# Recurrences of the first two batches on 16x16 blocks, with a block level on TensorE and layout changes by DVE transposes

## The chip, the cores and the metric

The kernel runs on one core of one Trainium2 chip. The metric is the device time in microseconds: the median over several runs of the same program. One of the executions is recorded by the hardware profiler, and every row quoted from the profile or the trace comes from that execution. PE is TensorE's matmuls (PEld its weight loads), DVE VectorE, ACT ScalarE, POOL GpSimd, and SP the engine whose queue issues all DMAs of this kernel (SPq).

## The reference

Two stages, in fp32. The first is a delta rule over 768 positions for 4 batches and 8 heads of dimension 48; the second is a feed-forward layer on its output (3072 tokens, 384 to 1024 to 384), with a SoLU activation and a layer norm.

```python
k_n = k / (np.linalg.norm(k, axis=-1, keepdims=True) + 1e-06)
for t in range(S):
    kt, vt, bt = (k_n[:, :, t], v[:, :, t], beta[:, :, t, None])
    y[:, :, t] = np.einsum('bhd,bhde->bhe', q[:, :, t], state)
    v_old = np.einsum('bhde,bhd->bhe', state, kt)
    state = state + bt[:, :, :, None] * np.einsum('bhd,bhe->bhde', kt, vt - v_old)
```
```python
h = x @ w_in
e = np.exp(h - h_max)
solu = h * e / (np.sum(e) + 1e-09)
ln = (solu - mu) / np.sqrt(var + 1e-06) * g_ln
out = ln @ w_out
```

## The kernel before

**Tiles.** The 768 positions are cut into 12 chunks of 64. A *unit* is one chunk for one pair of batch entries (two entries on 128 lanes, 8 heads side by side), so there are 24 units, numbered in the order in which the state passes through them. Within a chunk the recurrence is the inverse of a triangular 64x64 matrix per head and batch entry, made of the products of the keys (the gram). The inverses of several units are made together: what the title calls a batch (m in the code, `NB = 7` of them) holds two units (m = 0, chunk 0), four units (m = 1 to 5, two chunks) or two units (m = 6, chunk 11). Batch 2 therefore starts with unit 6.

**One batch.** `gram` multiplies a unit's keys with themselves and with the queries on PE (tiles gram and qk in PSUM, tag "fl", two buffers); ACT copies the gram to SBUF (g), DVE masks the queries' part (pm). g goes to DRAM (gd). `to_inv` gathers it back by strided DMAs into ginv, so that each of the 128 lanes holds one 32x32 diagonal block (lane = batch entry, half of the chunk, unit and head). `norms` takes the keys' norms with small DVE operations, `inv_begin` scales the blocks and keeps their triangle (DVE, then a select on POOL), and `inv_step` runs the recurrence, 30 steps of two elementwise operations (itmp, y) over the block. For m = 0 and 1 the columns of each step are divided between DVE (the first ten) and POOL; from m = 2 on POOL does all of it. `inv_end` copies y transposed on ACT (ginv again), stores both forms in DRAM (zd, xd) and gathers them back into the layout that PE needs (zt, gx, gy). `tlevel` with `block_level` joins two 32x32 inverses into a 64x64 one with small matmuls (mps, msb).

**One unit after that.** `chain` multiplies the state with keys and queries (kps, yps), forms the residual r, applies the inverse (ups, from zt) and updates the state (cps) and the output y. y times 64 is split into two fp16 parts (xh on ACT, xl on DVE), and each part is transposed by a DMA (xth, xtl). `moe_h` is 18 matmuls on the fp16 parts of x and w_in (h), the softmax-like activation, and two more DMA transposes (pth, ptl); `moe_out` is 24 matmuls with w_out's parts (ops), a correction and the store. The weights come as 8-byte floats: `to_f32` converts them by integer operations on DVE and products on POOL, six blocks of w_in and eight of w_out, and each block is split into two fp16 parts.

**What sets the order.** Nothing is issued as the Python runs. A `Recorder` collects all operations with a priority (the time given to `add` in the last part of the kernel, plus a shift), an assumed duration and their dependences. `Recorder.order` then plays the program through: an engine that is free takes, of the operations that are ready by the planner's clock, the one with the lowest priority value; a tile is taken from its ring (p1 to p10 are pools of 1 to 10 buffers per tag) when its first operation is placed. The resulting order per engine is fixed, and each engine works it off in order. SP is one such engine: the planner gives a DMA 5 ns per KB. Rings that matter here: kq and pm have ten buffers, kv four, the raw w_in blocks share three with pr, ginv, y and gx have two, and gy one. The gram of batch 2 is held behind the last level recorded before it (`last0`).

Of the kernel before, what the change touches and what calls it, by code (L numbers as in the profile page):

```python
# [20 lines left out]
CH = 1  # L21
SC = 64.0
# [265 lines left out]
class Queue:  # L288
# [17 lines left out]
def kernel(  # L306
# [128 lines left out]
    kqt, kvt, ztx, gxt = {}, {}, {}, {}  # L435
# [61 lines left out]

    def gram(m, u, t0):
# [3 lines left out]
        g = p2.tile([P, H, C], F32, tag="g", name=f"g_{ch}_{bp}")  # L502
# [26 lines left out]
    ginv, yt = {}, {}  # L529
    last0 = [None]  # L530

    def to_inv(m):
        gi = p2.tile([P, 32, 32], F32, tag="ginv", name=f"ginv_{m}")
        ginv[m] = gi
        for b in range(4):
            blk = b % 2
            for z in range(1 if len(units(m)) == 4 else 2):
                src = gdt[m].rearrange("t u h j -> t (u h) j")
                n = H * len(units(m))
                ls = slice(0, n)  # L540
                sp.dma_start(
                    kb=128, out=gi[32 * b + 16 * z : 32 * b + 16 * z + n],
                    in_=src[32 * b : 32 * b + 32, ls, blk * 32 : blk * 32 + 32].rearrange("j l i -> l j i"),
                )
# [384 lines left out]
```

## Time and profile before

| what | value |
|---|---|
| median of 3 runs | 512.82 us (512.18 to 515.02) |
| profiled execution | 512.04 us, of which the span is 510.2 us |
| mean granted TensorE clock | 0.92 |
| busy: PE, DVE, POOL, ACT | 368.2, 318.6, 294.0, 192.9 us |
| DMA | 72.21 MB, 142 GB/s in the mean |

The span runs from the first to the last instruction of the program; the 1.8 us around it are not seen in the trace. The recurrences are the groups named y and itmp; since a helper records every operation, nearly all rows carry the same line (L265), and groups are told apart by tile names. A row of the timeline has start, length, engine, line, operation, tiles and shapes, a count, and in brackets the idle time of the engine before it with what ended it.

### The profile page before, as it was taken

How to read it: one execution, taken by the hardware profiler on the slowest of the kernel's cores; microseconds unless marked ns; L12 is line 12 of the kernel's file. 1: busy time of each engine (PE TensorE's matmuls, PEld its weight loads, DVE VectorE, ACT ScalarE, POOL GpSimd, SP SyncE). 2: the span in 40 equal slices, each digit the busy share in tenths (PEclk: the TensorE clock that was granted, in tenths of full speed). 3: DMA queues.
4: the chain of work that ended last, by engine and by line, in shares of the span. 5: the costliest groups of instructions: out<-in, count | busy, mean ns of one | idle time of the engine just before them, and what ended most of it. 6: DMA issues, size and time to landing. Idle time of an engine off the chain costs nothing.

```text
span 510.2 us, 18246 instructions
## 1 busy us (share of the span) xinstructions
PE 368.2 (72%) x7744; PEld 233.9 (46%) x7744; DVE 318.6 (62%) x791; ACT 192.9 (38%) x382; POOL 294.0 (58%) x506
## 2 busy tenths in 40 slices
PE   3510070689579488997598997787969797899974
PEld 3410070455346345665366564444635464566532
DVE  3599999887884383655088664256597355455670
ACT  2210241465522143536144544224345345454450
POOL 3378385966558998984016886008989898100000
PEclk9999999877876699998799998898989899999998
DMA  8685662987989949977999587985656866744332
GB/s 212 159 255 98 155 169 65 161 171 174 172 162 165 179 113 160 168 135 161 189 165 144 145 162 151 160 162 95 107 118 144 145 114 128 131 64 99 73 68 61
DMA packets 180640, 72.21 MB, mean 142 GB/s; under 512 B 165520, under 2 KB 168976, under 8 KB 180560
## 3 DMA queue, kind: packets, MB, share of 16 engines
q1 hardware_dynamic: 180560, 71.06, 70.8%
q8 instruction: 60, 0.98, 0.9%
q14 instruction: 20, 0.16, 0.1%
HBM read 37.21 MB, written 16.52 MB: 105 GB/s over the span
## 4 chain that ended last, share of the span: by engine, by line
POOL 28%; PE 22%; DVE 19%; issue 10%; DMA 9%; SPq 7%; ACT 4%; POOLq 0%; DVEq 0%; ACTq 0%
POOL y L265 13%; POOL itmp L265 11%; PE h L265 7%; SPq L265 7%; PE ops L265 7%; DVE y L265 5%; DVE itmp L265 4%; DMA zt<-zd 3%; DMA ginv<-gd 3%; PE mps L265 2%; DVE wf L265 2%; DVE rst L265 1%; DVE st L265 1%; PE kps L265 1%; PE yps L265 1%
## 5 line engine op out<-in xcount | busy, mean ns | idle before, releaser
L265 POOL TENSOR_TENSOR y<-y,itmp 128x84 f32<-128x84 f32 (+16 forms) x190 | 100.7, 530 | 14.6
L265 POOL TENSOR_TENSOR itmp<-y,ginv 128x84 f32<-128x84 f32 (+16 forms) x190 | 93.3, 491 | 14.0
L265 DVE TENSOR_REDUCE st<-h 128x1 f32<-128x1024 f32 x24 | 29.3, 1222 | 87.5 <-PE h L265 82.2
L265 PE MATMUL qk<-kq 48*64 48x64 f32 x768 | 40.4, 269 | 24.9 <-DVE pm L265 15.6
L265 PE MATMUL gram<-kq 48*64 48x64 f32 x768 | 43.2, 270 | 18.8 <-DMA kq<-kq_dram 11.5
L265 POOL TENSOR_TENSOR st<-st,nhalf 128x1 f32<-128x1 f32 x24 | 13.2, 551 | 64.1 <-DVE st L265 64.1
L265 PEld LDWEIGHTS gram<-kq 48*64 48x64 f32 x768 | 37.5, 178 | 25.7 <-ACT g L265 6.3
L265 PEld LDWEIGHTS <-pth 128*128 128x128 f16 x384 | 37.6, 99 | 25.5 <-issue 1.7
L265 PE MATMUL h<-win_hi,xtl 128*128 128x512 f16 x144 | 45.4, 419 | 5.3 <-DVE pr L265 2.6
L265 PE MATMUL mps<-zt,gx 32*32 32x32 f32 x768 | 13.5, 205 | 48.6 <-issue 28.9
L265 PE MATMUL h<-win_lo,xth 128*128 128x512 f16 x144 | 46.7, 421 | 1.7 <-POOL win_lo L265 1.7
L265 PEld LDWEIGHTS qk<-kq 48*64 48x64 f32 x768 | 35.8, 178 | 25.3 <-DVE pm L265 16.1
L265 PEld LDWEIGHTS <-xth 128*128 128x128 f16 x288 | 28.4, 105 | 39.7 <-issue 14.8
L265 PE MATMUL ops<-wout_hi,ptl 128*128 128x384 f16 x192 | 38.7, 345 | 8.7 <-DMA ptl<-pl 6.8
L265 PE MATMUL h<-win_hi,xth 128*128 128x512 f16 x144 | 43.4, 411 | 0.0
L265 ACT ACTIVATE e<-h,st 128x1024 f32<-128x1024 f32 x24 | 26.7, 1114 | 38.0 <-DVE st L265 26.4
L265 POOL TENSOR_SCALAR_AFFINE_SELECT y<-y 128x1024 f32<-128x1024 f32 x7 | 9.4, 1346 | 53.5 <-DVE y L265 53.5
L265 DVE TENSOR_SCALAR st<-st 128x1 f32<-128x1 f32 (+1 forms) x216 | 35.5, 165 | 5.6
L265 PE MATMUL ops<-wout_lo,pth 128*128 128x384 f16 x192 | 36.9, 334 | 0.0
L265 PEld LDWEIGHTS mps<-zt,gx 32*32 32x32 f32 x768 | 10.1, 117 | 56.9 <-issue 34.8
L265 PE MATMUL ops<-wout_hi,pth 128*128 128x384 f16 x192 | 35.5, 326 | 0.0
L265 PE MATMUL cps<-u,kv 64*64 64x48 f32 x704 | 28.9, 235 | 9.1 <-ACT u L265 3.2
(94 smaller groups left out, 860.4 us busy)
## 6 DMA issues: line engine op xcount, KB each, us to landing
kq<-kq_dram SPq DMA_DIRECT2D x48, 192.0 KB, 4.5
kv<-kv_dram SPq DMA_DIRECT2D x24, 384.0 KB, 4.3
gd<-g SPq DMA_DIRECT2D x48, 128.0 KB, 3.3
out_dram<-oc SPq DMA_DIRECT2D x24, 192.0 KB, 2.2
zd<-y SPq DMA_DIRECT2D x7, 512.0 KB, 2.6
wi<-w_in_dram SPq DMA_DIRECT2D x6, 512.0 KB, 4.4
wo<-w_out_dram SPq DMA_DIRECT2D x8, 384.0 KB, 4.0
ginv<-gd SPq DMA_DIRECT2D x20, 128.0 KB, 4.2
```

Source lines behind the costliest of these rows:

```text
L265: fn(*[real(a) for a in args], **{k: real(a) for k, a in kw.items()})
```

## The change

For m < `SPLIT` = 2 the 32x32 block is worked as two 16x16 blocks, one on DVE and one on POOL at the same time (`blocks`), in 14 steps. The joining 16x16 block is made by PE: the gram is computed in three 32x32 parts, the layout changes gram to ginv, y to zt and ginv to gy are DVE transposes in place of stores to DRAM and gathers, and a new `small_level` joins two 16x16 inverses before `block_level` joins the 32x32 ones. From m = 2 on the recurrence stays on POOL with DRAM, but g is stored with one DMA instead of two; batch 6 zeroes ginv and gathers 16 lanes instead of 32 per quarter. The gram of batch 2 is not held any more. The two fp16 parts of x are written to one tile and transposed by one DMA. The planner now gives a DMA at least 550 ns and a DMA transpose at least 1,400 ns, and the priorities of the first two batches move: everything of batch 0 forward, the gram and loads of batch 1 right behind it, the kv loads of both ahead of w_in.

```diff
+SPLIT = 2
-        return self.rec.add(self.name, self.engine.dma_start, (), kw, kb * 5.0, 2000)
+        return self.rec.add(self.name, self.engine.dma_start, (), kw, max(550.0, kb * 5.0), 2000)
-        return self.rec.add(self.name, self.engine.dma_start_transpose, (), kw, kb * 5.0, 2000)
+        return self.rec.add(self.name, self.engine.dma_start_transpose, (), kw, max(1400.0, kb * 5.0), 2500)
...
     def gram(m, u, t0):
-        if m == 2:
-            rec.after = last0[0]
+                    if near:
+                        for r, a, b, o in ((0, lo, lo, lo), (32, up, up, lo), (32, up, lo, up)):
+                            pe.matmul(ns=25, out=gps_[C * b2 + r : C * b2 + r + 32, h, o], lhsT=kk[:, a], rhs=kk[:, b], ...)
+                    else:
+                        pe.matmul(ns=60, out=gps_[half(1 - b2), h], lhsT=kk, rhs=kk, start=True, stop=True)
+        if near:
+            hs = slice(H * u, H * u + H)
+            act.copy(out=gct[m][:, hs], in_=gps_[:, :, lo])
+            for r in (32, 96):
+                act.copy(out=gxt[m][0][r : r + 32, hs], in_=gps_[r : r + 32, :, up])
-        for b2 in range(2):
-            sp.dma_start(kb=128, out=gdt[m][half(b2), u], in_=g[half(1 - b2)])
+        sp.dma_start(kb=256, out=gdt[m][:, u], in_=g)
...
     def to_inv(m):
+        if m < SPLIT:
+            dve.transpose(ns=1900, out=gi.rearrange("l j i -> l i j"), in_=gct[m].rearrange("j l i -> j i l"))
+            return
...
+    def blocks(m):
+        return [(dve, slice(0, 16)), (gps, slice(16, 32))] if m < SPLIT else [(gps, slice(0, 32))]
     def inv_step(m, j):
-        parts = [(gps, 0, j)] if m > 1 else [(dve, 0, min(j, 10)), (gps, 10, j)]
+        for eng, q in blocks(m):
+            y, b = yt[m][:, q, q], ginv[m][:, q, q]
+            n = q.stop - q.start - 1 - j
...
     def inv_end(m):
+        if m < SPLIT:
+            act.copy(n=256, out=x1[:, 0:16, 16:32], in_=y[:, 0:16, 0:16].rearrange("p i j -> p j i"))
+            for q in (0, 16):
+                gps.memset(x1[:, q : q + 16, q : q + 16], 0.0)
+            dve.transpose(ns=1900, out=zz[:, :, 32:64].rearrange("p l i -> p i l"), in_=y.rearrange("l j i -> l i j"))
+            dve.transpose(ns=1900, out=xy[:, 0:1024].rearrange("p (l i) -> p i l", i=32), in_=x1.rearrange("l j i -> l i j"))
+            return
...
+    def small_level(u, nm, zz, z0, gx, xy):
+        with rec.atomic():
+            for l in range(H):
+                for r in lanes:
+                    pe.matmul(ns=25, out=mps[r, l], lhsT=xy[r, x : x + 32], rhs=zz[r, z0 + l, 48:64], start=True, stop=True)
+        act.mul(out=ssb, in_=mps, mul=-1.0)
+        with rec.atomic():
+            for l in range(H):
+                for r in lanes:
+                    pe.matmul(ns=25, out=zps[r, l], lhsT=xy[r, x : x + 32], rhs=ssb[r, l], start=True, stop=True)
+        dve.tensor_tensor(out=zz[:, zs, 48:64], in0=zz[:, zs, 48:64], in1=zps, op=ALU.add)
+        for r in lanes[::2]:
+            dve.transpose(out=gx[r], in_=zz[r, zs, 32:64])
+        for r in lanes[::2]:
+            act.copy(out=zz[r, zs, 0:32], in_=zz[r, zs, 32:64])
...
     def chain(m, u, tb, tu, tk):
-        for x, s in ((xl, "l"), (xh, "h")):
-            t = p2.tile([P, 3, P], F16, tag=f"xt{s}", name=f"xt{s}_{nm}")
-            sp.transpose(kb=96, out=t, in_=x)
+        x2 = p1.tile([P, 2, DM], F16, tag="x2", name=f"x2_{nm}")
+        sp.transpose(kb=192, out=t, in_=x2.rearrange("p a f -> p (a f)"))
...
-        add(once(-9, lambda bp=bp: load_kv(0, bp), lambda bp=bp: fill_v(0, bp)))
-        add(tlevel(0, bp, -12.9 + 0.1 * bp, -12.85 + 0.1 * bp))
+        add(once(-13.25, lambda bp=bp: load_kv(0, bp), lambda bp=bp: fill_v(0, bp)))
+        add(tlevel(0, bp, -12.9 + 0.1 * bp, -12.85 + 0.1 * bp), -2)
-    add(once(-13.4, lambda: norms(0)))
+    add(once(-13.4, lambda: norms(0)), -2)
-        add(load_w_out(i, -1 + 0.05 * i, 2.1 + 0.05 * i))
+        add(load_w_out(i, -0.6 + 0.05 * i, 2.1 + 0.05 * i))
-            tg = e - 9 + 0.9 * u if m > 1 else -11.2 + 0.05 * u
+            tg = e - 9 + 0.9 * u if m > 1 else -13.34 + 0.01 * u
-        add(inversion(m, tn + 0.6, e - 2.6 if m > 1 else -10))
+        add(inversion(m, tn + 0.6 if m > 1 else -12.97, e - 2.6 if m > 1 else -12.5))
```

More of the change, by code (lines that the diff above doesn't have):

```diff
@@ L501, in gram @@
         k = kqt[ch, bp]
-        g = p2.tile([P, H, C], F32, tag="g", name=f"g_{ch}_{bp}")
+        near = m < SPLIT
+        if near and u == 0:
+            gct[m] = p2.tile([P, 32, 32], F32, tag="y", name=f"gc_{m}")
+            if len(units(m)) == 2:
+                gps.memset(gct[m][:, 2 * H :], 0.0)
+            gxt[m] = p2.tile([P, 4 * H, 32], F32, tag="gx", name=f"gx_{m}"), None
+        g = None if near else p2.tile([P, H, C], F32, tag="g", name=f"g_{ch}_{bp}")
         pm = p10.tile([P, H, C], F32, tag="pm", name=f"pm_{ch}_{bp}")
@@ L534, in to_inv @@
         ginv[m] = gi
+        if m < SPLIT:
+            dve.transpose(ns=1900, out=gi.rearrange("l j i -> l i j"), in_=gct[m].rearrange("j l i -> j i l"))
+            moved[m] = rec.ops[-1]
+            return
+        if len(units(m)) == 2:
+            rec.after = moved[m]
+            dve.memset(gi, 0.0)
+            rec.after = None
+        n = H * len(units(m))
+        src = gdt[m].rearrange("t u h j -> t (u h) j")
         for b in range(4):
             blk = b % 2
[L537 to L544, printed above, removed]
+            r = 32 * (b ^ 2)
+            sp.dma_start(
+                kb=4 * n, out=gi[32 * b : 32 * b + n],
+                in_=src[r : r + 32, 0:n, blk * 32 : blk * 32 + 32].rearrange("j l i -> l j i"),
+            )
@@ L557, in inv_begin @@
         act.copy(n=32, out=y.rearrange("p j i -> p (j i)")[:, 0 : 32 * 32 : 33], in_=nb)
-        yt[m] = y
     def inv_step(m, j):
-        y, b = yt[m], ginv[m]
-        n = 31 - j
-        parts = [(gps, 0, j)] if m > 1 else [(dve, 0, min(j, 10)), (gps, 10, j)]
-        for eng, c0, c1 in parts:
-            if c1 <= c0:
-                continue
-            c = c1 - c0
-            tmp = p1.tile([P, 256], F32, tag=f"itmp{eng.name}", name=f"itmp_{m}_{j}_{c0}")
-            tv = tmp[:, 0 : c * n].rearrange("p (c i) -> p c i", i=n)
+        for eng, q in blocks(m):
+            y, b = yt[m][:, q, q], ginv[m][:, q, q]
+            n = q.stop - q.start - 1 - j
+            if n <= 0:
+                return
+            tmp = p1.tile([P, 256], F32, tag=f"itmp{eng.name}", name=f"itmp_{m}_{j}_{q.start}")
+            tv = tmp[:, 0 : j * n].rearrange("p (c i) -> p c i", i=n)
@@ L621, in block_level @@
         msb = p1.tile([P, n, 32], F32, tag=f"msb{n}", name=f"msb_{nm}")
-        act.mul(out=msb, in_=mps, mul=-1.0)
+        for r in [slice(0, P)] if len(groups) > 1 else [slice(C * b2, C * b2 + 32) for b2 in range(2)]:
+            act.mul(out=msb[r], in_=mps[r], mul=-1.0)
         yield t1
@@ L641, in tlevel @@
         gx, gy = gxt[m]
-        gx, gy = (x[:, H * u : H * u + H] for x in (gx, gy))
+        gx = gx[:, H * u : H * u + H]
+        if m < SPLIT:
+            small_level(u, f"{m}_{u}", ztx[m], H * u, gx, gy)
+            yield from block_level(u, f"{m}_{u}", ztx[m], H * u, [(range(8), gx, gx, 0)], t0, t1)
+            return
+        gy = gy[:, H * u : H * u + H]
         yield from block_level(u, f"{m}_{u}", ztx[m], H * u, [(range(4), gx, gx, 0), (range(4, 8), gx, gy, 32)], t0, t1)
@@ L836 @@
         for u in range(nu):
-            tg = e - 9 + 0.9 * u if m > 1 else -11.2 + 0.05 * u
+            tg = e - 9 + 0.9 * u if m > 1 else -13.34 + 0.01 * u
             ch, bp = units(m)[u]
-            add(once(tg - 0.9 if m > 1 else -11.8, lambda ch=ch, bp=bp: load_kq(ch, bp)))
+            add(once(tg - 0.9 if m > 1 else -13.36, lambda ch=ch, bp=bp: load_kq(ch, bp)))
             add(gram(m, u, tg))
```

107 lines of the change are left out of this document (64 added, 43 removed).

## The prediction, made before the result was known

> **What bounds the kernel now.** I read the page first (span, PE's slices, chain), then the busy times in six stretches, then POOL's instructions in order of time. The page gives the span, the slices of PE, and the chain of work that ended last:
>
> ```profile
> span 510.2 us, 18246 instructions
> PE   3510070689579488997598997787969797899974
> POOL 28%; PE 22%; DVE 19%; issue 10%; DMA 9%; SPq 7%; ACT 4%; POOLq 0%; DVEq 0%; ACTq 0%
> ```
>
> A slice is 12.75 us. PE is nearly empty in the first eight (0 to 102 us) and mostly at 7 to 9 tenths after that. The stretches (columns: length, then busy time of PE, PEld, DVE, ACT, POOL, granted clock, DMA share, GB/s) put numbers on it:
>
> ```profile
> 0.00:60.00 60.00, 13.98 (x384) 12.10 (x384) 42.88 (x116) 10.23 (x15) 29.92 (x61) 1.00 0.72 175
> 60.00:102.00 42.00, 18.32 (x483) 14.76 (x485) 38.05 (x83) 12.81 (x27) 33.46 (x54) 0.95 0.66 136
> 102.00:144.00 42.00, 32.67 (x862) 20.25 (x859) 34.48 (x82) 22.25 (x52) 24.06 (x20) 0.77 0.89 171
> 144.00:190.00 46.00, 33.09 (x566) 21.38 (x565) 27.80 (x62) 11.84 (x19) 40.52 (x70) 0.74 0.82 156
> 190.00:432.00 242.00, 207.45 (x4597) 129.04 (x4595) 136.87 (x351) 103.01 (x212) 159.19 (x287) 0.94 0.77 143
> 432.00:510.00 78.00, 62.72 (x866) 36.41 (x866) 38.49 (x104) 32.75 (x60) 6.82 (x17) 0.98 0.43 89
> ```
>
> Up to 102 us PE works 32 us, DVE 81, POOL 63: the head is two recurrences, one after the other, on DVE and POOL. From 190 on PE works 270 of 320 us. Four events mark the way (timeline rows of POOL, then rows of the chain):
>
> ```profile
> 31.63 0.22 POOL L265 TENSOR_TENSOR itmp<-y,ginv 128x20 f32<-128x20 f32 x1
> 47.80 0.24 POOL L265 TENSOR_TENSOR y<-y,itmp 128x20 f32<-128x20 f32 x1
> 103.29 1.15 POOL L265 TENSOR_TENSOR win_lo<-wf,win_hi 128x512 f16<-128x512 f32 x1
> 147.20 0.55 POOL L265 TENSOR_TENSOR itmp<-y,ginv 128x30 f32<-128x30 f32 x1
> 187.64 0.26 POOL L265 TENSOR_TENSOR y<-y,itmp 128x30 f32<-128x30 f32 x1
> ```
> ```profile
> 103.27 3.53 PE h L265 x8
> 205.02 1.06 PE ups L265 x32
> ```
>
> POOL's share of recurrence 0 lasts from 31.6 to 48.0. The last block of w_in is split at 104.4, and the first unit's h ends at 106.8, right behind it. Recurrence 2, on POOL alone, ends at 187.9 (y_2). The first unit that needs it, unit 6, starts its ups at 205.0. I take y_2 as the milestone: from there on the order is a loop with no fixed date (a unit's end frees the pm and kq tiles of the unit ten later, whose gram feeds a recurrence, which feeds a unit), so what is gained at y_2 is carried to the end.
>
> **The change, part by part.** The sum follows POOL's queue from the start of recurrence 0 to y_2, since the change alters what stands on it.
>
> When it can start. These rows of DVE and ACT give the prices:
>
> ```profile
> 12.45 0.58 ACT L265 COPY g<-gram 128x512 f32<-128x512 f32 x1 [3.24 <-PE qk L265]
> 56.39 0.21 DVE L265 STREAM_TRANSPOSE nrt<-nrn 128x32 f32<-128x32 f32 x1
> 57.54 1.22 DVE L265 TENSOR_TENSOR ginv<-ginv,nn 128x1024 f32<-128x1024 f32 x1
> 49.62 0.21 DVE L265 TENSOR_TENSOR itmp<-y,ginv 128x50 f32<-128x50 f32 x1
> L265 DVE TENSOR_TENSOR itmp<-y,ginv 128x30 f32<-128x30 f32 (+26 forms) x60 | 21.7, 361 | 2.0
> L265 ACT COPY ginv<-y 128x1024 f32<-128x1024 f32 x7 | 13.8, 1972 | 50.1 <-issue 19.8 <-POOL y L265 18.5 <-DVE y L265 11.7
> ```
>
> The second gram of batch 0 is copied out by 13.0. Now norms(0) has priority -15.4, ahead of the pm at -13.5, so some 13 small DVE operations, each like the 0.21 of the small transpose and a gap (3 us together) run first and hold the PSUM tile. PE has 64 matmuls where it had 32 (0.9 more by the 0.45 of 32 small ones in a row quoted further down, which counts each fp32 matmul twice; 1.6 with an allowance for changes of form), and ACT makes three smaller copies for one (0.6): 18.2. The DRAM way is gone (gd, eight gathers, gx). In its place stands one DVE transpose of 128x1024 with strided operands. No such row is there: the dense 1024-element operation at 1.22 and ACT's strided copy at 1.97 bound it, and I take 1.9, the nearer in layout: 20.1. Half-block products (256 elements, 0.42 each on DVE, between the 0.21 of 50 and the 1.22 of 1024) and the select bring it to **21.5**; it was 31.6.
>
> What POOL then does until y_2:
>
> ```profile
> 32.56 0.26 POOL L265 TENSOR_TENSOR y<-y,itmp 128x38 f32<-128x38 f32 x1
> 32.90 0.28 POOL L265 TENSOR_TENSOR itmp<-y,ginv 128x54 f32<-128x54 f32 x1
> 33.26 0.28 POOL L265 TENSOR_TENSOR y<-y,itmp 128x54 f32<-128x54 f32 x1
> L265 POOL TENSOR_SCALAR_AFFINE_SELECT y<-y 128x1024 f32<-128x1024 f32 x7 | 9.4, 1346 | 53.5 <-DVE y L265 53.5
> L350 POOL TENSOR_SCALAR_AFFINE_SELECT mask<-mask 64x64 f32<-64x64 f32 x2 | 0.5, 234 | 0.1
> L265 POOL TENSOR_SCALAR wc_i<-wc_i 128x512 f32<-128x512 f32 x6 | 12.5, 2083 | 14.8 <-ACT wc_i L265 14.3
> L265 POOL TENSOR_TENSOR wf<-wf,wc_i 128x512 f32<-128x512 f32 x6 | 7.8, 1300 | 5.0 <-DVE wf L265 4.8
> L265 POOL TENSOR_TENSOR win_lo<-wf,win_hi 128x512 f16<-128x512 f32 x6 | 6.9, 1161 | 0.9 <-ACT win_hi L265 0.7
> L265 POOL TENSOR_SCALAR wc_o<-wc_o,g_sb 128x384 f32<-128x384 f32 x8 | 12.9, 1613 | 9.7 <-ACT wc_o L265 9.2
> L265 POOL TENSOR_TENSOR wg<-wg,wc_o 128x384 f32<-128x384 f32 x8 | 8.3, 1040 | 0.8 <-DVE wg L265 0.5
> L265 POOL TENSOR_TENSOR kv<-kv,nrt 128x384 f32<-128x384 f32 x22 | 18.3, 845 | 23.8 <-DMA kv<-kv_dram 22.3 <-DVE rst L265 1.4
> ```
>
> - Recurrence 0: a 16x16 block takes steps j = 1 to 14 of two operations over j(15-j) elements, 14 to 56. From start to start POOL needs 0.34 to 0.36 for 38 to 54 elements, so 28 x 0.335 = 9.4. DVE's 28 at 0.25 (0.21 and a gap) are 7 and hidden under it.
> - Recurrence 1: the same 9.4, two half products (0.63 each, between the 0.28 of 54 elements and the 845 ns of 384), two selects of 256 elements (between 0.23 and 1.35; 0.5, nearer the small one): 11.6. Memsets of both: eight, taken at 0.3 each like a step of 54 elements, 2.4.
> - w_in, six blocks: 12.5 + 7.8 + 6.9 = 27.2. w_out, eight: 21.2. Six fills of kv: 5.1.
> - Recurrence 2: the full select 1.3, then 40.4 from 147.2 to 187.9 less a w_out block counted above: 39.4.
>
> Together 117.6, so y_2 at 139.1 if POOL never waits. It will: recurrence 1 needs four more grams through two PSUM tiles whose pm waits behind DVE's steps, then norms(1) (18 small operations, 4 us), while w_in's DVE parts have the lowest priority. Bounds: 0, and 26, which is what POOL stood idle of the 84 us from 60 to 144 (33.46 and 24.06 busy in the stretches). I take 13, the middle: **y_2 at 152.1 instead of 187.9, a gain of 35.8**, between 23 and 49. Two things move at the same time. The m = 2 gram is no longer held behind the last level, so its gather is done early and recurrence 2 does not wait for it. And unit 0's h, bound by w_in, comes after 21.5 + 9.4 + 11.6 + 2.4 + 27.2 and some waiting, at about 77 instead of 107; the 98 us from there to unit 6's ups become at most as many, which gives 175 against 152.1 + 17.1 = 169 from y_2 (205.0 less 187.9 is 17.1). The two agree.
>
> The level on blocks of 16 adds 64 small matmuls, a copy, an add, two transposes and two copies per unit, for six units: a chain of some ten short operations at 0.2 to 0.5 each, about 4 us. It replaces zd, xd, zt, gx and gy through DRAM. PE is idle there; without that cover it is 1.8 us of PE per unit (four blocks at 0.45), 11 in all.
>
> SP's queue: one transposing DMA of x instead of two (24 issues fewer), one gd store instead of two from m = 2 on (18 fewer). Rows of SP and of the landing times:
>
> ```profile
> 138.20 1.27 SPq L265 DMA_TRANSPOSE xth<-xh  x1
> 140.87 1.34 SPq L265 DMA_TRANSPOSE pth<-ph  x1
> xth<-xh SPq DMA_TRANSPOSE x24, 3.4
> pth<-ph SPq DMA_TRANSPOSE x24, 4.0
> ```
>
> An issue costs the same for 1024 columns as for 384, so the merged one of 768 should cost 1.3 and land in 3.4 to 4.0. Against that, the h of a unit now waits for both halves at once; it starts with the low one and needs both anyway. At y_2 18 units are still to come, 18 x 1.27 = 23 us of issue, and the gd stores of three batches bring it to some 28. SPq is only 7% of the chain, so most of these issues lie beside other work: I take a quarter, **7** (0 to 28).
>
> Loads that move on SP: the kv of batch 0 and the first two of batch 1 now stand ahead of w_in, 4 x 384 KB, which at the 175 GB/s of the first stretch is 9 us. POOL took up w_in near 20 us before and takes it up behind recurrence 0 near 31 now, so this is hidden; without that cover it is 9. The w_out loads (-1 to -0.6) stay behind the kq of batch 2, as before. The planner's new floors (550 and 1,400 ns) alter only the order.
>
> Sum: 510.2 - 35.8 - 7 = 467.4 of span. The profiled execution took 512.0, 1.8 around its span: 469.2, and the median of the runs is 0.8 above that execution: **470**. Ends: 510.2 - 23 - 0 = 487 and 510.2 - 49 - 28 = 433 of span, the latter only if both go best.
>
> One rule speaks against the change. The Trainium skill ("TensorEngine Tiling (Array Packing)", Key Properties) says that changing the tiling mode drains TensorE, and the new gram alternates outputs of 32 and 64 columns. The trace shows forms changing here:
>
> ```profile
> 223.30 0.45 PE L265 MATMUL mps<-zt,gx 32*32 32x32 f32 x32
> 223.68 0.25 PE L265 MATMUL kps<-st,kq 48*64 48x48 f32 x1
> L265 PE MATMUL gram<-kq 48*64 48x64 f32 x768 | 43.2, 270 | 18.8 <-DMA kq<-kq_dram 11.5
> ```
>
> The kps begins at 223.68, 0.07 before the block of mps ends at 223.75, so this change of form waited for no full drain; the sum above holds none. By that rule every one of some 32 changes per unit would wait for the matmul in flight, a mechanism that stands below as a rival.
>
> **The rivals.** (1) *The head stays as long.* The blocks get shorter, but w_in's conversion waits for DVE and ACT as before, so POOL idles as long as before: 190 less the 128 busy of the first four stretches is 62, less the 21.5 ahead of recurrence 0 is 40 instead of 13. y_2 at 179, gain 9, and 510.2 - 9 - 7 + 1.8 = 496. For it: DVE is busy for 81 of the first 102 us, and norms, pm and the six units' new levels all stand before w_in in priority. Against it: DVE's parts of the two recurrences were 60 products, 21.7 us, and as many sums; they become 56 and 56 at 0.21.
>
> (2) *The middle tightens as well.* Recurrence 2 is finished early against its need, SP has air, and the 320 us from 190 on, which hold 270 us of PE work, go at 93% of PE instead of 84%: 290, 30 less, of which 7 are in the sum already: 447. For it: the chain has 28% POOL, so recurrences pace the middle; the changed planner gives an SP transpose 1,400 ns where its rows show 1,270. Against it: recurrences 3 to 6 are as long as before, and the DMA share is 0.77 in that stretch.
>
> (3) *TensorE drains at each change of form.* A full drain is at most the 0.27 us of a gram matmul; 32 of them are 8.6 us per unit. The two units of batch 0 start recurrence 0 later by 17; the four of batch 1 lie under POOL's w_in. The time would be 470 + 17 = 487. Against it stands the overlap at 223.68.
>
> (4) *Slower: recurrence 2 gets ahead of w_in.* Without the brake on the m = 2 gram its steps are ready early, and POOL works in one order, fixed ahead. If they stand before the last win_lo, unit 0's h ends at 21.5 + 9.4 + 11.6 + 2.4 + 1.3 + 39.4 + 27.2 + 13 = 126 instead of 106.8. From that h to the end it takes the 403 us of before, less 7: 522 of span, 524. It turns slower once more than 30 us of recurrence 2 (107 less 77) come first. For it: the planner lets an engine take what is ready. Against it: w_in has priority -8 to -7.5, recurrence 2 has 1.2 to 3.4, and only a gap in w_in lets it in.
>
> **How the numbers follow.** Forecast 0.60 (470; its own range 452 to 489 from the bounds, the lowest corner left to rival 2), rival 1 0.13, rival 2 0.14, rival 3 0.08, rival 4 0.05. The range 441 to 498 takes in the forecast, rival 3, and most of rivals 2 and 1. A measurement of this kernel tells about 0.5% (2.6 us) from no change. Faster: forecast, 2, 3 and 0.10 of rival 1, that is 0.92; within 0.5%: the 0.03 of rival 1 in which SP's relief is nothing too; slower: rival 4, 0.05.
>
> **What would show it.** Right: no DMA of gd, ginv, zd or gx before the third batch; POOL's recurrence steps of 14 to 56 elements in two runs of about 9.4 us, the first from about 21.5; the last win_lo near 74 instead of 104; y_2 near 152; ups of unit 6 near 170; from there some 300 us to the end, with 24 SP transposes of x near 1.3 us. Wrong: win_lo or y_2 where they were (rival 1); long stretches of recurrence 2 before the last win_lo (rival 4); grams of the first two batches of 8 us and more (rival 3); a stretch from y_2 to the end under 295 us (rival 2). A strided DVE transpose of more than 3 us or a merged x transpose that lands after more than 6 us would break terms of the sum without a rival that names them.

## The result

The changed kernel is slower: 534.67 us median (533.0 to 540.76) against 513.3 (512.18 to 515.02), a ratio of 1.0435 with an interval of 1.0342 to 1.0528. The forecast was 470 (441 to 498), with a chance of 0.05 for slower. The profiled execution is the longest of the four (540.76, span 538.8), which is why its span grows by 28.6 and the median by 21.

The page of the changed kernel (span, busy tenths of PE, DVE and POOL in slices of 13.47 us, chain by engine):

```profile
span 538.8 us, 20386 instructions
PE   6999997379878678689969898796977798899985
DVE  3020448998698838525618766248586455555570
POOL 4042224899641899888400788403899898200000
POOL 36%; PE 34%; issue 11%; DVE 10%; DMA 5%; SPq 2%; ACT 2%; POOLq 0%; DVEq 0%; ACTq 0%
```

PE was nearly empty in the first 100 us before. Now its first seven slices stand at 6 to 9 tenths, while DVE and POOL are idle for much of that time; PE's share of the chain went from 22% to 34%. The same six stretches as in the prediction (length, then busy time of PE, PEld, DVE, ACT, POOL, granted clock, DMA share, GB/s), the first four of them:

```profile
0.00:60.00 60.00, 52.69 (x558) 39.72 (x558) 14.75 (x47) 7.51 (x17) 16.31 (x50) 1.00 0.45 118
60.00:102.00 42.00, 35.65 (x790) 29.66 (x788) 27.12 (x65) 12.97 (x31) 19.20 (x30) 1.00 0.25 76
102.00:144.00 42.00, 29.78 (x1005) 23.37 (x1006) 35.12 (x61) 18.95 (x43) 37.01 (x40) 1.00 0.31 79
144.00:190.00 46.00, 34.82 (x879) 23.58 (x879) 38.10 (x94) 19.97 (x36) 23.30 (x33) 0.81 0.86 175
```

In the first 60 us PE works 52.7 us instead of 14.0, DVE 14.8 instead of 42.9. What PE does there is the six grams of batches 0 and 1 (groups of PE up to 82 us: count, busy time, mean ns; then its timeline, three periods of it and the last):

```profile
L266 PE MATMUL qk<-kq 48*64 48x64 f32 x192 | 45.2, 337 | 0.0
L266 PE MATMUL gram<-kq 48*32 48x32 f32 x576 | 40.7, 244 | 8.1 <-DMA kq<-kq_dram 4.1 <-DVE pm L266 2.4 <-ACT gx L266 1.6
```
```profile
14.02 0.42 PE L266 MATMUL gram<-kq 48*32 48x32 f32 x6
14.37 0.47 PE L266 MATMUL qk<-kq 48*64 48x64 f32 x2
14.77 0.42 PE L266 MATMUL gram<-kq 48*32 48x32 f32 x6
15.12 0.47 PE L266 MATMUL qk<-kq 48*64 48x64 f32 x2
15.52 0.42 PE L266 MATMUL gram<-kq 48*32 48x32 f32 x6
15.88 0.47 PE L266 MATMUL qk<-kq 48*64 48x64 f32 x2
...
80.48 0.47 PE L266 MATMUL qk<-kq 48*64 48x64 f32 x2
```

One pair (three gram matmuls and one qk, each counted twice) has a period of 0.75 us; the 16 pairs of a unit take 12.1 us. Before, a unit took 2.1, its gram and qk lying side by side (the kernel before, one unit, 16.4 to 18.7 us):

```profile
L265 PE MATMUL gram<-kq 48*64 48x64 f32 x32 | 2.1, 314 | 0.7 <-ACT g L265 0.7
L265 PE MATMUL qk<-kq 48*64 48x64 f32 x32 | 2.0, 314 | 0.0
```

Six units in a row fill PE from 3.9 to 80.9. What that does to the others (DVE's rows up to the first conversion of w_in, then SP's gap, then POOL):

```profile
29.32 0.69 DVE L266 TENSOR_TENSOR pm<-qk,mask 128x512 f32<-128x512 f32 x1 [12.18 <-PE qk L266]
29.93 2.02 DVE L266 STREAM_TRANSPOSE ginv<-gc 128x1024 f32<-128x1024 f32 x1
...
42.23 0.69 DVE L266 TENSOR_TENSOR pm<-qk,mask 128x512 f32<-128x512 f32 x1 [9.36 <-PE qk L266]
55.14 0.69 DVE L266 TENSOR_TENSOR pm<-qk,mask 128x512 f32<-128x512 f32 x1 [12.22 <-PE qk L266]
68.05 0.69 DVE L266 TENSOR_TENSOR pm<-qk,mask 128x512 f32<-128x512 f32 x1 [5.76 <-PE qk L266]
68.66 0.42 DVE L266 TENSOR_SCALAR wf<-wi 128x512 int32<-128x512 int32 x1
...
80.99 0.69 DVE L266 TENSOR_TENSOR pm<-qk,mask 128x512 f32<-128x512 f32 x1 [6.46 <-PE qk L266]
```
```profile
17.52 5.64 SPq L266 DMA_DIRECT2D kq<-kq_dram  x5
70.61 0.35 SPq L266 DMA_DIRECT2D wi<-w_in_dram  x1
```
```profile
32.95 0.51 POOL L266 TENSOR_SCALAR_AFFINE_SELECT y<-y 128x256 f32<-128x256 f32 x1 [26.06 <-DVE y L266]
...
93.66 1.82 POOL L266 TENSOR_SCALAR_AFFINE_SELECT y<-y 128x256 f32<-128x256 f32 x2
...
127.79 1.16 POOL L266 TENSOR_TENSOR win_lo<-wf,win_hi 128x512 f16<-128x512 f32 x1
...
218.33 0.26 POOL L266 TENSOR_TENSOR y<-y,itmp 128x30 f32<-128x30 f32 x1
```

DVE works in order. Its pm of each unit waits 6 to 12 us for PE's qk, and w_in's conversion stands behind the third pm of batch 1: it begins at 68.7. SP stands still from 23 to 70.6 as well: next in its order is the fourth block of w_in, which needs the raw buffer of a converted one. On POOL the first select of recurrence 0 stands at 33.0 and its first step at 36.2 (predicted 21.5), those of recurrence 1 at 93.7 and 96.8; the last block of w_in ends at 129.0 (before 104.4, predicted 74), y_2 at 218.6 (before 187.9, predicted 152.1). From y_2 to the end it is 320.2 us, before 322.3: all the loss lies ahead.

### The profile page after: what moved, and what is told of

It is laid out like the page before. It is cut to its first block, busy times and chain, and to the rows that moved or that the text cites. A ratio compares the mean times of both kernels' runs of the same rounds, so it can differ in the third digit from the quotient of the medians.

```text
span 538.8 us, 20386 instructions
## 1 busy us (share of the span) xinstructions
PE 448.8 (83%) x8896; PEld 297.7 (55%) x8896; DVE 308.1 (57%) x752; ACT 201.0 (37%) x406; POOL 287.4 (53%) x499
## 4 chain that ended last, share of the span: by engine, by line
POOL 36%; PE 34%; issue 11%; DVE 10%; DMA 5%; SPq 2%; ACT 2%; POOLq 0%; DVEq 0%; ACTq 0%
POOL y L266 16%; POOL itmp L266 15%; PE qk L266 7%; PE gram L266 7%; PE h L266 7%; PE ops L266 5%; PE ups L266 2%; PE sps L266 2%; PE mps L266 2%; SPq L266 2%; POOL st L266 2%; DMA kq<-kq_dram 2%; POOL kv L266 1%; DVE wf L266 1%; DVE y L266 1%
## 5 line engine op out<-in xcount | busy, mean ns | idle before, releaser
L266 POOL TENSOR_TENSOR y<-y,itmp 128x84 f32<-128x84 f32 (+14 forms) x178 | 92.7, 521 | 13.5
L266 POOL TENSOR_TENSOR itmp<-y,ginv 128x84 f32<-128x84 f32 (+14 forms) x178 | 90.0, 505 | 13.0
L266 PE MATMUL h<-win_hi,xt 128*128 128x512 f16 x288 | 86.1, 418 | 0.6 <-DVE pr L266 0.6
L266 PE MATMUL qk<-kq 48*64 48x64 f32 x768 | 71.8, 276 | 9.7 <-DVE pm L266 9.4
L266 PE MATMUL gram<-kq 48*32 48x32 f32 (+1 forms) x1152 | 69.2, 250 | 9.7 <-DMA kq<-kq_dram 4.1
L266 PEld LDWEIGHTS gram<-kq 48*32 48x32 f32 (+1 forms) x1152 | 53.0, 154 | 30.7 <-DMA kq<-kq_dram 4.3
L266 PEld LDWEIGHTS <-xt 128*128 128x128 f16 x432 | 41.3, 105 | 50.3 <-issue 14.9
L266 PE MATMUL h<-win_lo,xt 128*128 128x512 f16 x144 | 47.4, 426 | 0.0
L266 PE MATMUL ups<-r,zt 64*64 64x48 f32 x704 | 29.7, 243 | 12.8 <-DVE r L266 11.0
L266 DVE SCALAR_TENSOR_TENSOR pl<-pr,st,ph 128x1024 f16<-128x1024 f32 x24 | 33.3, 1386 | 7.1 <-ACT ph L266 6.5
```

The costliest lines, as they stand in the source:

```text
L266: fn(*[real(a) for a in args], **{k: real(a) for k, a in kw.items()})
```

## The experiments

**The changes of form.** Theory D: TensorE waits at each change between outputs of 32 and of 64 columns. Four kernels: the changed one with its matmuls sorted by unit, sorted by groups of four pairs, with one form only, and the kernel before with the forms alternated.

```diff
 # sorted by unit (2 changes)
-for h2 in range(0, H, 2):
+for h2, part in [(h2, p) for p in ("gq" if near else ["gq"]) for h2 in range(0, H, 2)]:
     # the three 32x32 of gram only in part "g", the qk only in part "q"
 # sorted by groups (8 changes)
-    for h, b2 in hb[2 * h2 : 2 * h2 + 4]:
+    for part, (h, b2) in [(p, x) for p in ("gq" if near else ["gq"]) for x in hb[2 * h2 : 2 * h2 + 4]]:
 # one form (no change of form)
-for r, a, b, o in ((0, lo, lo, lo), (32, up, up, lo), (32, up, lo, up)):
-    pe.matmul(ns=25, out=gps_[C * b2 + r : C * b2 + r + 32, h, o], lhsT=kk[:, a], rhs=kk[:, b], ...)
+pe.matmul(ns=60, out=gps_[half(b2), h], lhsT=kk, rhs=kk, start=True, stop=True)
...
-act.copy(out=gct[m][:, hs], in_=gps_[:, :, lo])
+for r in range(0, P, 32):
+    act.copy(out=gct[m][r : r + 32, hs], in_=gps_[r : r + 32, :, up if r % C else lo])
...
 # the kernel before, alternated, batches 0 and 1
-pe.matmul(ns=60, out=gps_[half(1 - b2), h], lhsT=k[dims(b2), h, 0], rhs=k[dims(b2), h, 0], ...)
+for r, c in ((0, 0), (32, 0), (32, 32), (0, 32)):
+    pe.matmul(ns=25, out=gps_[C - C * b2 + r : C - C * b2 + r + 32, h, c : c + 32], lhsT=kk[:, r : r + 32], rhs=kk[:, c : c + 32], ...)
```

> The changed kernel, with the 48 gram matmuls of a unit of batches 0 and 1 ahead of its 16 qk matmuls: 2 changes of form per unit instead of 32, the same matmuls. In the changed kernel a unit's gram and qk hold TensorE for 12.1 us. Theory D (TensorE waits out its matmul in flight at each change between the 32-column and the 64-column outputs): 16 qk are half of the 2.0 us that 32 of them took before, 48 small ones are 0.8 by the 1.05 of 64 in the level on blocks of 16, so a change costs (12.1 - 1.8) / 32 = 0.32, and a unit takes 1.8 + 2 x 0.32 = 2.4 us; the head gets shorter by up to 58 us, and the time is 470 to 495 us. Rival S (the small matmuls of 48 rows are slow in themselves, in whatever order): a unit still takes 8 us or more, time 520 or more. Rival O (the grams get short, but norms, pm and the six units' levels, which stand on DVE ahead of w_in's conversion, keep the last win_lo at 110 us or later): a unit takes 2.4 us, time 515 or more.

> The same, sorted only within each group of four pairs: 8 changes of form per unit. Theory D: 1.8 + 8 x 0.32 = 4.4 us per unit, so six grams are 12 us longer than with 2 changes, and the time lies 5 to 15 us above the kernel sorted by unit. Rival S: 8 us or more per unit. Rival O: 4.4 us per unit, the time as when sorted by unit.

> The changed kernel with one 64x64 matmul per pair for the gram of batches 0 and 1, in the half of the partitions in which its qk stands, instead of three of 32x32; ACT then copies the four row blocks out separately. No change of form is left in these grams. Theory D: about 2.0 us per unit, as the grams before, up to 4 if two matmuls into the same half cannot overlap; time 465 to 490, at or below the kernel sorted by unit. Rival S: the same 2.0 us, which alone would not tell it from D. Rival O: 515 or more.

> The kernel before, with each 64x64 gram matmul of batches 0 and 1 cut into four of 32x32 and the qk left as they are, pair by pair: nothing is added but 48 small matmuls and 32 changes of form per unit. Theory D: 1.05 + 1.0 + 32 x 0.32 = 12.3 us per unit instead of 2.0; batch 0's two units begin recurrence 0 later by 20, and batch 1's four delay recurrence 1 by 0 to 41, time 533 to 560. Rival S: 8 us or more per unit as well; D and S differ in the two kernels with sorted matmuls. If neither holds and the price came from elsewhere in the changed kernel: 2.5 us per unit, time 513 to 517.

Measured: sorted by unit 499.2 us (ratio 0.9724, 0.9673 to 0.9775), by groups 501.7 (0.9763, 0.9722 to 0.9803), one form 495.9 (0.9642, 0.9604 to 0.9679), the kernel before with alternated forms 558.7 (1.0875, 1.0841 to 1.0910). PE's first unit sorted, then the start of that by groups, then the alternated kernel before:

```profile
4.77 1.92 PE L266 MATMUL gram<-kq 48*32 48x32 f32 x90 [0.57 <-DMA kq<-kq_dram]
6.62 1.97 PE L266 MATMUL qk<-kq 48*64 48x64 f32 x32
```
```profile
6.13 0.67 PE L266 MATMUL gram<-kq 48*32 48x32 f32 x24
6.73 0.69 PE L266 MATMUL qk<-kq 48*64 48x64 f32 x8
7.35 0.67 PE L266 MATMUL gram<-kq 48*32 48x32 f32 x24
```
```profile
13.96 0.42 PE L265 MATMUL gram<-kq 48*32 48x32 f32 x8
14.31 0.47 PE L265 MATMUL qk<-kq 48*64 48x64 f32 x2
14.71 0.42 PE L265 MATMUL gram<-kq 48*32 48x32 f32 x8
```

The very same matmuls take 3.9 us per unit with 2 changes (1.92 and 1.97), 4.9 with 8 (four periods of 1.22), 12.1 with 32 (16 of 0.75). Between 2 and 32 changes a change costs (12.1 - 3.9) / 30 = 0.27 us, between 2 and 8 it is 0.17. In the alternated kernel before the period is again 0.75, though there are four small matmuls in it and not three: the changes set it, not the work. Two other causes fall as well. The granted clock is 1.00 in the first 60 us of all these kernels. And in the one-form kernel gram and qk alternate just as often, into the same two PSUM tiles, and a unit takes 4.2 to 4.7 us: alternating alone is not what costs. So the mechanism of theory D holds in all four, and rival S (small matmuls slow in themselves) falls; so does rival O, with the last win_lo at 95.4 when sorted by unit (110 or later was said). The times that theory D gave held only in the fourth: 499.2 for 470 to 495, 2.5 us more by groups for 5 to 15, 495.9 for 465 to 490, 558.7 for 533 to 560. The price was expected at 0.32 because 1.8 us was put for the matmuls themselves, which take 3.9.

Not all of the 0.75 us lies at the two changes. From start to start 0.17 goes by from the last gram to the first qk and 0.24 from the last qk to the next gram; 0.16 lies between the two passes of the one qk and 0.19 within the six of gram. Sorted by unit, starts of qk lie 0.05 apart in the mean, since neighbouring pairs overlap there. That the loss of this overlap is part of the 0.27 fits these numbers; it was not tested by itself.

The one-form kernel still differs from the kernel before in where the gram goes, so the next kernel puts it into the other half of the partitions than its qk (the copies then read from the half opposite):

```diff
-pe.matmul(ns=60, out=gps_[half(b2), h], lhsT=kk, rhs=kk, start=True, stop=True)
+pe.matmul(ns=60, out=gps_[half(1 - b2), h], lhsT=kk, rhs=kk, start=True, stop=True)
...
-    act.copy(out=gct[m][r : r + 32, hs], in_=gps_[r : r + 32, :, up if r % C else lo])
+    act.copy(out=gct[m][r : r + 32, hs], in_=gps_[r ^ C : (r ^ C) + 32, :, up if r % C else lo])
```

> The one-form kernel (495.9 us) with the gram's 64x64 output in the other half of the partitions than its qk, as in the kernel before. In the one-form kernel a unit's gram and qk took 4.2 to 4.7 us with both in one half, in the kernel before 2.0 us with the two in different halves. If the halves work side by side: about 2.0 to 2.9 us per unit again, the half products of recurrence 0 begin some 2 us ahead of the 21.8 they have, and the time is 488 to 494. If these grams no longer set anything: 2.0 us per unit and 494.5 to 497.5.

Measured: 490.65 us, ratio 0.9553 (0.9524 to 0.9582), with its variant "norms first" below (490.2), from which it can't be told apart, the fastest kernel of the study. The groups of PE up to 82 us, one form first, quadrants second:

```profile
L266 PE MATMUL gram<-kq 48*64 48x64 f32 x256 | 28.0, 315 | 12.0 <-DVE pm L266 5.5 <-DMA kq<-kq_dram 4.1 <-ACT gx L266 2.4
```
```profile
L266 PE MATMUL gram<-kq 48*64 48x64 f32 x256 | 18.8, 315 | 17.1 <-DVE pm L266 8.4 <-ACT gx L266 4.2 <-DMA kq<-kq_dram 4.1
```

With both outputs in one half a unit takes 4.2 to 4.7 us, in different halves 2.5 to 2.9 (the first and the last of the six, which hardly wait); a run of 62 of the 64 records takes 3.7 and 2.0. The time fell as expected when the halves work side by side (488 to 494), though it is one of several things that moved: recurrence 0's first step came 1.8 us earlier, at 24.2, and unit 2's ups 4.0 us earlier.

**Batch 2's grams and the brake.** Free of changes of form the kernel stands at 491 to 496, not at 470: y_2 is at 178.5 (one form) and 173.1 (quadrants), not at 152. Two trials on the one-form kernel, each a part of the prediction's claim that recurrence 2 does not wait for its gather any more:

```diff
 # grams of batch 2 due earlier
-tg = e - 9 + 0.9 * u if m > 1 else -13.34 + 0.01 * u
+tg = e - 9 + 0.9 * u if m > 2 else -7.4 + 0.05 * u if m > 1 else -13.34 + 0.01 * u
 # the brake put back, in gram() and at the end of block_level()
+if m == 2:
+    rec.after = last0[0]
...
+last0[0] = rec.ops[-1]
```

> The one-form kernel with the grams of batch 2 (and their loads) due right behind w_in, at -7.4 in place of -3 to -0.3. In the one-form kernel recurrence 2's select waits 7.1 us for DVE's y, which waits for the gather from DRAM that SP issues at 117.7; POOL stood idle for 29 us of the 155 from recurrence 0 to y_2. Theory G (the late grams of batch 2 hold recurrence 2): select at 126 to 129 instead of 132.6, time 489 to 493. Rival (w_out's conversion and the order of DVE fill that place anyway, or the grams wait for their PSUM tiles whatever their due time): select at 131 or later, 494 to 498.

> The one-form kernel with the brake put back: the grams of batch 2 again wait for the latest recorded level, as in the kernel before. By the prediction's step (without the brake the gather is done early and recurrence 2 does not wait for it) putting it back would delay recurrence 2 and cost up to 8 us: 498 to 504. Rival (those grams come late without the brake as well, since the third and fourth begin only at 106 and 109): 494 to 498, select of recurrence 2 within 2 us of 132.6.

Measured: 496.6 and 495.5, both the same as 495.9; recurrence 2's select at 133.0 and 132.2 against 132.6. Neither matters, and the rival's range was right both times. Recurrence 2's select waits 7.1 us in the one-form kernel (first row below; the others are the selects of recurrences 3 and 4), 11.3 in the changed kernel and 8.2 before. It waits for DVE's y; DVE's work on the gathered blocks begins at 125.4, after 1.4 us of waiting for the gather, and takes 7 us. So the step "recurrence 2 does not wait for it" was wrong; the brake made no difference.

```profile
132.61 1.27 POOL L266 TENSOR_SCALAR_AFFINE_SELECT y<-y 128x1024 f32<-128x1024 f32 x1 [7.09 <-DVE y L266]
178.43 1.27 POOL L266 TENSOR_SCALAR_AFFINE_SELECT y<-y 128x1024 f32<-128x1024 f32 x1
257.50 1.27 POOL L266 TENSOR_SCALAR_AFFINE_SELECT y<-y 128x1024 f32<-128x1024 f32 x1 [7.67 <-DMA kq<-kq_dram]
```

**SP: the merged transpose of x and the planner's floors.** The merge is taken out of the one-form kernel, put alone into the kernel before, and the floors are taken out with and without the merge.

```diff
 # two transposes (and the reverse of it in the kernel before)
-t = p2.tile([P, 6, P], F16, tag="xt", name=f"xt_{nm}")
-sp.transpose(kb=192, out=t, in_=x2.rearrange("p a f -> p (a f)"))
+for x, s in ((xl, "l"), (xh, "h")):
+    t = p2.tile([P, 3, P], F16, tag=f"xt{s}", name=f"xt{s}_{nm}")
+    sp.transpose(kb=96, out=t, in_=x)
...
 # no floors
-... max(550.0, kb * 5.0), 2000)
+... kb * 5.0, 2000)
-... max(1400.0, kb * 5.0), 2500)
+... kb * 5.0, 2000)
```

> The one-form kernel with the x of each unit transposed by two DMAs again, as in the kernel before. The prediction's term for the relief of SP's queue was 7 us (0 to 28), most of it these 24 issues of 1.3 us. If the term holds: 500 to 504, nearly all of it behind y_2. If the issues lie beside other work: 494 to 498. If two smaller DMAs land sooner, so that h starts earlier: 490 to 494.

> The kernel before with one change alone: x of a unit transposed by one DMA of 768 columns instead of two of 384. With the blocks in place (one-form kernel) the merge was worth 513.1 - 495.9 = 17.2 us, all of it behind y_2. Theory M (the relief of SP's queue is worth that by itself, since the gathers of recurrences 3 and 4 stand behind x on SP): 495 to 501, and recurrence 4's select at 257 to 262 instead of 270.9. Theory B (the blocks gain about 17 of their own, and two transposes only lose it again because of the new planner's order): 510 to 514. The prediction's term, 7: 505 to 508.

> The one-form kernel (x merged) with the planner's costs for SP as before: no floors of 550 and 1,400 ns, and 2,000 ns to a transposing DMA's landing. Theory M: the number of issues decides, not the planner's order, 494 to 499. Rival P (the floors give the order in which SP's gathers come ahead of x): 503 or more.

> The one-form kernel with two transposes of x and the planner's old costs for SP: of the change only the blocks, the other loads' places and the missing brake are left. Theory M (what the blocks gain in the head is given back behind y_2, because the gathers wait on SP): 508 to 515, as with the floors. Theory B (the floors together with two transposes made a bad order, and the blocks gain by themselves): 495 to 503.

| kernel | x in one DMA | x in two DMAs |
|---|---|---|
| before | 514.1 (0.9983, 0.9959 to 1.0007) | 513.2 to 514.9 |
| one form, floors | 495.9 (0.9642) | 513.1 (0.9953, 0.9924 to 0.9983) |
| one form, no floors | 495.4 (0.9623) | 499.3 (0.9698, 0.9662 to 0.9733) |

With two transposes the one-form kernel is 17 us slower, above all three ranges that were given for it, and that comparison by itself (theory M) misleads. The kernel without floors, 495.4, came as theory M said too. But the merge is worth nothing in the kernel before, and 4 us on the blocks without floors. The floors do nothing with one transpose and cost 14 us with two: the planner then finds an order with recurrence 4's select at 268.7 instead of 262.2 without the floors and 257.5 with the merge. Theory B holds: without merge and floors, what is left of the change (the blocks above all, with the one gd store, the moved loads and the missing brake) is worth 514 - 499 = 15 us, the merge 4. On the kernel with quadrants the floors count for nothing either:

> The kernel with quadrants (490.7 us) with the planner's old costs for SP. On the one-form kernel they made no difference (495.4 against 495.9): 489 to 493. If they matter together with the earlier start: 484 to 488, or 494 or more.

Measured: 492.5 (0.9587, 0.9543 to 0.9633); with floors 490.65.

**Does a gain at y_2 reach the end?** The quadrants kernel with three, four and all seven batches on blocks (which takes recurrence 2's gather and most of its POOL work away):

```diff
-SPLIT = 2
+SPLIT = 3   # then 4, then 7
```

> The one-form kernel with quadrants (490.7 us; y_2 at 172.5), with batch 2 on blocks of 16 as well: no gather from DRAM for recurrence 2, and POOL's part of it about 10 us, as in recurrences 0 and 1, instead of 44. Theory Y (y_2 is the milestone and its gain is carried to the end): y_2 at 130 to 140, time 452 to 465. Rival E (recurrences 3 to 6, which still gather and run on POOL, and PE at 84% pace what follows, so that a gain at y_2 is mostly lost): y_2 as early, time 475 to 490. Rival A (what stands ahead of recurrence 2 holds y_2): y_2 at 160 or later, time 485 to 491.

> The same with four batches on blocks. Theory Y: nothing more is gained at y_2, 452 to 465 as with three. Rival E: each recurrence taken off POOL gains some 5 to 15 us more, 465 to 480.

> The same with all seven batches on blocks: POOL has 7 x 10 us of recurrences instead of 2 x 10 + 5 x 44, TensorE gets 18 levels of about 2.1 us more (384 + 38 = 422 us of work), DVE 310 + 5 x 13 = 375. Rival E (POOL's recurrences pace the middle): 440 to 465, the least of the three. If TensorE and DVE become the bound: 465 to 490. By theory Y alone: 452 to 465.

Measured: 500.2 (0.9744, 0.9708 to 0.9780), 510.4 (0.9943, 0.9910 to 0.9976), 534.8 (1.0410, 1.0373 to 1.0446). With three batches recurrence 2 ends at 134.0 on DVE (on POOL at 132.5), 39 us before the 173.1 of the quadrants kernel, and the kernel is 9.5 us slower. Every range that was given for these three kernels was missed; rival E, that the gain is mostly lost behind y_2, is the nearest, but a loss of 9.5 us was in none. POOL after its last step of recurrence 2, and its next select (for recurrence 3), with three batches; then that select in the quadrants kernel:

```profile
132.32 0.22 POOL L266 TENSOR_TENSOR y<-y,itmp 128x14 f32<-128x14 f32 x1
...
169.92 1.26 POOL L266 TENSOR_SCALAR_AFFINE_SELECT y<-y 128x1024 f32<-128x1024 f32 x1 [15.55 <-DVE y L266]
```
```profile
173.06 1.26 POOL L266 TENSOR_SCALAR_AFFINE_SELECT y<-y 128x1024 f32<-128x1024 f32 x1
```

Of 39 us, 3 are left at the next recurrence. Its gather from DRAM is issued at 155.4, later than in the quadrants kernel (147.7); that the grams ahead of it wait for kq tiles which units give back is read from the code and was not tested. So y_2 is not the milestone. With all seven PE works 428.8 us and DVE 376.1, about as expected (422 and 375); PE is 53% of the chain, DVE 26% and POOL 2%. By the chain the bound has moved to PE and DVE. How much of the added time is work and how much order or changes of form among the levels' small matmuls was not tested.

**What does the end follow?** Over the kernels so far the last win_lo went with the end (398 to 410 us ahead of it in most), so the last three kernels move w_in and recurrence 1 against each other, all on the quadrants kernel:

```diff
 # w_in first; "w_in mostly" has -12.6 + 0.01 * i in place of -12.995 + 0.0005 * i
-add(load_w_in(i // 2, i % 2, -11.5 if i < 2 else -11.0, -8 + 0.1 * i))
+add(load_w_in(i // 2, i % 2, -13.24, -12.995 + 0.0005 * i))
 # batch 1's norms ahead of batch 0's levels
-add(tlevel(0, bp, -12.9 + 0.1 * bp, -12.85 + 0.1 * bp), -2)
+add(tlevel(0, bp, -12.9 + 0.1 * bp, -12.85 + 0.1 * bp))
```

> The kernel with quadrants (490.7 us; last win_lo at 91.1, recurrence 1 on POOL from 59.0 to 69.4, ups of unit 2 at 93.3), with the loads of w_in at -13.24 and its conversion due ahead of batch 1's norms, so that all six blocks of w_in stand ahead of recurrence 1 on POOL. The last win_lo should come at 62 to 70 and recurrence 1 begin some 15 us later than now. Theory W (the end follows the last win_lo by about 398 us): 462 to 470. Rival U (the end follows recurrence 1, on which 22 of the 24 units depend): 500 to 508. Between: the early h of units 0 and 1 fills what PE has idle until unit 2 comes, 483 to 492.

> The same with w_in's conversion due a little later (-12.6), so that its last block stands among recurrence 1. Last win_lo at 75 to 85, recurrence 1 some 10 us later than in the kernel with quadrants. Theory W: 473 to 485. Rival U: 498 to 504. Between: 485 to 492.

> The kernel with quadrants (490.7 us; recurrence 1 on POOL from 59.0, ups of unit 2 at 93.3, end of the span 395.6 behind them), with batch 0's levels not ahead of batch 1's norms on DVE any more (their offset of -2 in priority removed). POOL waits there for 8.9 us (44.9 to 53.9, for the levels and the norms), and recurrence 1 should begin 4 to 8 us earlier. Theory U (the end follows unit 2): unit 2's ups at 85 to 90, time 483 to 487. Rival (the units 0 and 1, whose levels come later, or w_in, hold the end): unit 2's ups as early, time 489 to 493.

Measured: w_in first 504.3 (0.9790, 0.9764 to 0.9816), w_in mostly 518.0 (1.0036, 1.0006 to 1.0066), norms first 490.2 (0.9520, 0.9484 to 0.9556). Theory W falls: the last win_lo came 16 us earlier, at 75.1, and the kernel got 14 us slower. Theory U, that the end follows recurrence 1, gave 500 to 508 for it, and that holds; w_in mostly lies above every range that was given. What went with the end is the ups of unit 2, the first unit that needs recurrence 1 (rows of PE: before, changed, quadrants, w_in first, norms first):

```profile
109.70 1.14 PE L265 MATMUL ups<-r,zt 64*64 64x48 f32 x32 [0.31 <-DVE st L265]
```
```profile
131.06 1.95 PE L266 MATMUL ups<-r,zt 64*64 64x48 f32 x32
```
```profile
93.32 1.94 PE L266 MATMUL ups<-r,zt 64*64 64x48 f32 x32
```
```profile
108.08 1.95 PE L266 MATMUL ups<-r,zt 64*64 64x48 f32 x32
```
```profile
91.74 0.74 PE L266 MATMUL ups<-r,zt 64*64 64x48 f32 x20
```

From there to the end of the span: 400.5, 407.7, 395.6, 395.9 and 397.8 us; 396.5 with one form, 397.0 with the merge alone in the kernel before. It is no law: sorted by groups it is 402.9, with two transposes of x 412.6, with four batches on blocks 418.6, with all seven 435.8. So the ups of unit 2 tells the time of the end only as long as the middle stays as it is. Nor is it shown to be the cause: in w_in first the selects of recurrences 2 and 3 came 15 and 13 us later as well. In w_in mostly unit 2's ups stands at 108.05, as in w_in first, and the time is 14 us longer, 407.9 from there to the end: there recurrence 2 (119 to 178 us) got in among w_out, seven of whose eight blocks came only at 139 to 167 us. Norms first shows another limit of theory U: recurrence 1 began 7.3 us earlier (51.7), but unit 2's ups only 1.6 (both theories had put it at 85 to 90), and the time stayed: DVE copied unit 0's state, which unit 2's kps need, at 80.3 instead of 69.5, and those kps began at 89.2 instead of 88.6. Unit 2 needs recurrence 1 and unit 0, and DVE, busy for 36 to 38 of the 42 us from 60 to 102 in these two, works for both and for w_in. Whether a freer DVE would move it was not tried.

## Why the prediction was wrong

- **The step that failed** is "the sum above holds none": no price for changes of form, but for the 0.7 us of allowance in the start of recurrence 0. The runs showed 0.27 us per change, 12.1 us per unit where the same matmuls with 2 changes take 3.9; the kernel takes 534.7 us with 32 changes, 499.2 with 2 and, with one form, 495.9. The row that the prediction went by (kps at 223.68, 0.07 before mps ends at 223.75) has the same overlap as the changes that cost: in the changed kernel qk begins at 14.37, the gram ahead of it ends at 14.02 + 0.42 = 14.44. The profile models the ends of matmuls, and here the same overlap stands at a change that cost; so an overlap of ends does not rule out a wait. The distance of starts shows it. In the records behind those rows the last gram matmul starts at 14.201 and the first qk at 14.368, 0.17 us; back, from qk to gram, it is 0.24. Sorted by unit, starts lie (1.92 - 0.24) / 89 = 0.02 us apart in gram and (1.97 - 0.31) / 31 = 0.05 in qk, the length of the last matmul taken off. In the kernel before the last mps starts at 223.562, the kps at 223.683: 0.12 us against 0.006 to 0.03 within the block. A price of 0.1 could have been read there, 32 x 0.1 = 3 us per unit, less than half of the 8.2 that it was. The Trainium skill ("TensorEngine Tiling (Array Packing)", Key Properties) says that a change of mode, unlike a change of tile, drains TensorE. The runs agree that a change of form costs time (0.17 and 0.24 us between starts) and a change of tile does not (in the quadrants kernel gram and qk alternate with starts 0.007 us apart); that it is a drain, no run shows.
- **Rival 3 had the mechanism and the price, and missed the place.** Its sign, grams of 8 us and more, is what the trace shows. It said 8.6 us per unit, 32 times 0.27; measured are 12.1 - 3.9 = 8.2 for 30 changes. That its 0.27 comes out to the digit is partly luck: it was the length of a gram matmul, taken as a bound. Beside it the matmuls themselves take 1.9 us more than the 2.0 of before, where the sum had 0.9. That the four grams of batch 1 lie under w_in was wrong: w_in could not run under them, since its conversion stands behind their pm on DVE. So not only two units' worth of delay (17) counted but that of four to five: against the one-form kernel a unit is 7.4 to 7.9 us longer, the changed kernel lies 534.7 - 495.9 = 39 us above it, and its unit 2's ups 131.1 - 97.3 = 34 later.
- **Start of recurrence 0**: without changes of form its first step on POOL came at 24.2 (quadrants) and 26.0 (one form) for 21.5 predicted. The first select came at 21.0 and 22.8; behind it POOL had two half products, a second select and a fill of kv to do, 3.2 us that the sum put elsewhere or left out. The strided DVE transpose took 1.90 to 2.08 us for 1.9.
- **Recurrences 0 and 1**: 9.6 and 10.5 us on POOL (one form) for 9.4 each. DVE's part is 28 products and 28 sums for both together; the "56 and 56" of rival 1 counts them twice. The "40.4 from 147.2 to 187.9" is 40.7. All of POOL's work from that first select to y_2 (one form) was 127 for 117.6, with the gaps between short operations, and **its idle time 29 us for 13**. This is the second thing that the sum had wrong: y_2 at 178.5 for 152.1 even without changes of form. Before it was 31: the middle between 0 and 26 was taken where the kernel before already showed the value. Rival 1 had y_2 at 179 and the time at 496; without the changes of form that is the one-form kernel (178.5 and 495.9). So close a hit is partly luck: it had 40 us idle and 117.6 of work, and took y_2 for the milestone.
- **y_2 as milestone**: wrong, though 320.2 and 322.3 us from y_2 to the end look like it. Three batches on blocks gained 39 us at y_2 and lost 9.5 at the end. The two traces fit several milestones that moved together; only runs that move them apart decide. Unit 2's ups fits better: 109.7 before, 97.3 with one form, 12 us, and 4 behind it make the 16 us of span.
- **SP's relief, 7 (0 to 28)**: its larger part, the merged transpose, was worth 4 on the blocks and 0 in the kernel before. A merged transpose mostly took 1.21 to 1.32 to issue and landed after 3.7 us (median, changed kernel), as predicted (1.3; 3.4 to 4.0).
- **The brake and the floors** at nothing: right with one transpose. **Rivals 2 and 4** did not happen in the changed kernel; what rival 4 described shows in w_in mostly, with w_out in w_in's place. The 0.05 for a slower kernel stood for rival 4 alone, so the kernel became slower by a way to which the prediction gave no chance of that.

## What to carry to other kernels

Group the small matmuls of TensorE by the shape of their outputs, or give them one shape even where half the result is not needed: here 0.17 to 0.27 us per change made 3.9 us of matmuls into 12.1, and a gram of one form turned a loss of 4.4% into a gain of 3.6%, with the halves side by side 4.5%. When you cost such a change from a trace, compare starts, not ends. And before you make an event the milestone of a sum, ask what else moved with it: a rest of the same length behind one event in two traces does not show that the end follows it.

## What the runs showed of the hardware that was not expected

- A change between fp32 matmuls with weights of 48x32 and of 48x64, the 48 rows being the same, puts 0.17 us (narrow to wide) and 0.24 us (wide to narrow) between the starts; in close alternation it came to 0.27 per change.
- Two fp32 matmuls with outputs of 64x64 that lie in different halves of the partitions ran side by side, 2.0 us for the 62 records of a unit in a row; with both in one half it was 3.7. The Trainium skill ("TensorEngine Tiling (Array Packing)", Key Properties) says that different tiles run in parallel, and the trace agrees.
- ACT copied 32 rows of a PSUM tile to rows 64 partitions away in the same kernel that gained 5 us, so no DMA is needed to put the quadrants in order.
